# Float16 scores from the second group of batch 0 on, and a new written order of instructions

## The chip, the cores and the metric

The kernel runs on one core of one Trainium2 chip. The metric is the device time of one execution in microseconds (us). Three executions of the kernel before took 1048.6, 1049.95 and 1049.99 us; the median is 1049.95 us.

Five engines work side by side, each with an instruction stream of its own: PE (TensorE, matrix products into PSUM), DVE (VectorE), ACT (ScalarE), POOL (GpSimd) and SP (SyncE, which here issues most DMAs). An instruction waits for others by semaphores. PEld rows are PE's weight loads.

## The reference

Attention with pooled keys, then a soft mixture of experts over all tokens:

```python
kv_pool = kv.reshape(B, H // r, r, W // r, r, C).mean(axis=(2, 4))
k = v = kv_pool.reshape(B, -1, C) @ w_sr
s = (q @ k.transpose(0, 2, 1)) / sqrt(C);  a = softmax(s);  x = a @ v
logits = x @ phi                          # x is [B * N, 128], phi is [128, 32]
d = softmax over the tokens of logits;  slot_input = d.T @ x
slot_out[e] = relu(slot_input[e] @ w1[e]) @ w2[e]     # 8 experts, 4 slots each
out = softmax over the slots of logits @ slot_out
```

There are B = 4 batches of N = 12288 queries with C = 128 channels, and 768 pooled keys for each batch. All inputs and outputs are float32, and the queries are large, so scores and weights are computed in two parts, a high one and a low one that holds the rest.

## The kernel before, in words

The queries are cut into 96 blocks of 512, 24 for each batch, and into groups of 4 blocks (2048 queries), 6 for each batch. The last group is split 3 and 1. One block goes through these steps:

- ACT writes the high part of the block's queries (`q_hi`, L604 as float32r, L610 as float16), POOL the low part (`q_lo`, L615).
- PE computes the scores of 768 keys by 512 queries in 6 tiles, each as the sum of 3 products: high by high, low by high, high by low (`qk`, L625 to L627), 18 in all.
- DVE reduces them to one maximum for 32 queries (`rowmax1`, L643), folds the tiles (`rowmax2`, L653, L655), PE spreads the result (L663), DVE reduces again and transposes (L668, L673, the tile `mb`). There is one L673 in each block.
- DVE subtracts the maximum (`sub`, L681, into the tile `t`), ACT takes the exponential twice, as float16 (L689, `phi`) and as float32 (L693), POOL subtracts the two (`plo`, L698).
- PE multiplies by the values (L724, L725 with the high weights, L733 with the low ones), ACT brings the result to SBUF (L743).

After the four blocks of a group, group work computes logits, their running maximum over the tokens, and the slots' sums (`group_ops`, with L914 on PE, L827 on DVE, L877 and L892 on POOL). The row softmax over the slots has a maximum (L933), a subtraction, an exponential and a sum (`k_sum`, L950). For groups up to `SUMS` the sum stands in the loop, in two halves; for later ones it stands at the end, in one piece.

In batch 0 all scores are float32r (`HB = 1`: the first batch). From batch 1 on they are float16. That asks for more: the keys are divided by a power of two near their magnitude, and each group's queries too. For each group ACT makes two passes for the magnitude (`q_abs`, L534) and two that scale the queries in place (`q_mul`, L558), PE and DVE turn the magnitude into a power of two (`q_s_mm`, `q_s_g`), POOL multiplies it with the keys' (`q_sig`), and the exponentials and L655 take their scale from the tile that results (`qsg`) and not from a constant.

The keys of batches 1 to 3 are prepared while the batch before is computed (`kv_ops`: L453, L457, L462, L475, L496, L576, L577, L585), in the second half of its blocks.

The order on PE, DVE, ACT and POOL is written out by hand, by a planner in the program (`Plan`): each step is entered with an engine, a cost in us, a latency, a priority (the time at which it is wanted), what it depends on, and the buffers that it takes and gives back. The planner lets the engines run on those costs and picks at each step the ready one with the lowest priority; a `fill` step is held back for a gap until its due time, and a `hot` step is waited for a little. What it emits is the static order of each engine. `PER` is the planned time of one block, `HEAD` that of the first, and `act(n)` and `dve(n)` are costs by columns. The costs are no waits: on the chip each instruction starts when its semaphores allow.

At the end the experts' products are made, the last sums and reciprocals are finished, and 25 MB of output go out by SP's queue (`o_out`, `o_dma`).

Of the kernel before, what the change touches and what calls it, by code (L numbers as in the profile page):

```python
# [20 lines left out]
P = 128  # L21
# [6 lines left out]
HB = 1  # L28
# [8 lines left out]
SPARE = 0.02  # L37

# [4 lines left out]
class Plan:  # L43
# [170 lines left out]
def attention_then_soft_moe(ctx: ExitStack, tc: tile.TileContext, qT, kv0, kvT, w_sr, w_srT, phi, w1, w2, outT):  # L214
# [127 lines left out]
    PER = 9.8  # L342
# [11 lines left out]
    SUMS = 6  # L354
    JOIN = (0, AHEAD, 6, 8, 10, 13, 16, 19, EARLY)
    KV0 = 12.5
# [41 lines left out]
    def kv0_mm(h, c, first, end):  # L398
        if h == 0 and first:
            kT[0] = (  # L400
                bp.tile([P, NK], F32R, tag="khi", name="khi_0"),
                bp.tile([P, NK], F32R, tag="klo", name="klo_0"),
            )
# [156 lines left out]
    def sig(i):  # L560
        return SCALE if i < HB * BPB else QS[i // BPG]["s"][:, 0:1]
# [36 lines left out]
    def q_hi(i):  # L598
        if i < HB * BPB:
# [12 lines left out]
    def q_lo(i):  # L612
        hi, lo = qsp[i]
        eng = nc.gpsimd if i else nc.vector
        eng.tensor_tensor(out=lo, in0=q_src(i), in1=hi if i >= HB * BPB else hi.bitcast(F32), op=ALU.subtract)  # L615


    def qk(i, t):
        khi, klo = kT[i // BPB]
# [29 lines left out]
    def rowmax2(i):  # L649
# [6 lines left out]
            out=rq, in0=r1.unsqueeze(1).broadcast_to([P, NQD, NBK]), scalar=-math.log(PK) / SCALE if i < HB * BPB else QS[i // BPG]["s"][:, 1:2],  # L656
# [463 lines left out]
    kv_s(0, VBASE, VSTEP, m, [])  # L1120

    def group_ops(g):
# [22 lines left out]
        def bg(f=1.1):  # L1145
            return dve(n512) if fast else f * n512 / 512
# [4 lines left out]
        def go(name, eng, cost, dep, f, acq=(), use=(), path=None, fill=False):  # L1151
            k[0] += 1
            due = base + step * k[0] + (LATE if g else 4.0) if fill and not fast else None
            o[name] = op(eng, cost, 0.08, base + step * k[0], dep, lambda: f(g), acq=list(acq), use=[xl] + list(use) if name in ("0", "1v", "1l", "7m") else list(use), slack=0.0 if fast else SL, raw=0.05 if fast else 0.14, fill=due)
# [3 lines left out]
        else:  # L1158
            go("0", small, sm_(1), deps, g0)
            go("0r", "DVE", 0.21, [o["0"]], g0r, fill=True)  # L1160
            go("1u", small, sm_(1), [o["0r"]], g1u)
            go("1l", big, bg(), [o["1u"]], g1l)
        if g <= FAST:
            go("1v", small, sm_(2), [o["0r"]], g1v)
        if fast:
            go("2a", "DVE", dve(n512), [o["1l"]], lambda g: g2(g, 0, n16))
        else:
            go("2a", "DVE", dve(n512 // 2) + 0.06, [o["1l"]], lambda g: g2(g, 0, n16 // 2), fill=True)
            go("2a", "DVE", dve(n512 // 2) + 0.06, [o["2a"]], lambda g: g2(g, n16 // 2, n16), fill=True)
# [102 lines left out]
    for i in range(NB):  # L1272
# [5 lines left out]
        if o == 0 and g + 1 < NG and g + 1 >= HB * GPB:  # L1278
# [16 lines left out]
        ops["ql", i] = op("POOL" if i else "DVE", 1.28 if i else 0.65, 0.1, T0 - 0.9 * PER if i else -400.0, [a], lambda i=i: q_lo(i), use=[("q", g), ("qs", i)])  # L1295
        kd = [ops["k", b, x] for x in range(2 if b else 3)]
        for t in range(NT):
            u = t // 2
            if i == 0 and t == NT - 2:
# [4 lines left out]
                "PE", 3 * (0.2165 if f16_ else 0.2315), 0.17, T0 - QKP + 0.65 * t, [ops["ql", i]] + kd[: (1 if t < KSPLIT // P else 2) if b else t // 2 + 1] + ([ops["qk", i, t - 1]] if t else [ops["qk", i - 1, NT - 1]] if i else []),  # L1304
# [423 lines left out]
```

## Time and profile before

| | |
|---|---|
| profiled execution | 1051.33 us |
| its span, first to last instruction | 1049.5 us |
| median of the executions without profile | 1049.95 us |
| PE busy | 1013.4 us, 97% |
| DVE busy | 967.2 us, 92% |
| ACT busy | 892.6 us, 85% |
| POOL busy | 873.3 us, 83% |
| mean granted PE clock | 0.992 |

A row of instructions gives line, engine and operation, what is written from what, the shapes, and the count; behind it stand the busy time, the mean length in ns, and the idle time of the engine just before, with what ended it. Matrix products are pipelined: one that is listed with 0.38 us can start 0.22 us after the one before, so that the distance of starts, not the length, tells what it costs. The same holds in part for the other engines, whose instructions overlap a little at their ends. A stretch is given in us from the span's start.

### The profile page before, as it was taken

How to read it: one execution, taken by the hardware profiler on the slowest of the kernel's cores; microseconds unless marked ns; L12 is line 12 of the kernel's file. 1: busy time of each engine (PE TensorE's matmuls, PEld its weight loads, DVE VectorE, ACT ScalarE, POOL GpSimd, SP SyncE). 2: the span in 40 equal slices, each digit the busy share in tenths (PEclk: the TensorE clock that was granted, in tenths of full speed). 3: DMA queues.
4: the chain of work that ended last, by engine and by line, in shares of the span. 5: the costliest groups of instructions: out<-in, count | busy, mean ns of one | idle time of the engine just before them, and what ended most of it. 6: DMA issues, size and time to landing. Idle time of an engine off the chain costs nothing.

```text
span 1049.5 us, 24780 instructions
## 1 busy us (share of the span) xinstructions
PE 1013.4 (97%) x10297; PEld 774.2 (74%) x10297; DVE 967.2 (92%) x1487; ACT 892.6 (85%) x1185; POOL 873.3 (83%) x550
## 2 busy tenths in 40 slices
PE   8999999999999999999999999999999999998994
PEld 5788889888777767777777777777777777777452
DVE  6999999999999999999999999999999999997794
ACT  3777787889999998999999999999999999885473
POOL 0789999898899998899999999898998899985340
PEclk9999999999999999999999999999999999999997
DMA  9334411102116411111125303111100110113498
GB/s 370 116 65 98 101 37 51 42 1 102 42 16 146 101 34 54 42 31 71 42 46 117 90 13 86 42 61 42 42 7 36 42 41 2 42 41 122 179 417 366
DMA packets 15728, 89.16 MB, mean 85 GB/s; under 512 B 1664, under 2 KB 1920, under 8 KB 9344
## 3 DMA queue, kind: packets, MB, share of 16 engines
q1 hardware_dynamic: 11728, 69.47, 17.7%
q0 software_dynamic: 3312, 17.70, 8.9%
q8 instruction: 81, 1.33, 0.5%
q10 hardware_dynamic: 576, 0.41, 0.1%
q14 instruction: 31, 0.25, 0.1%
HBM read 58.87 MB, written 25.17 MB: 80 GB/s over the span
## 4 chain that ended last, share of the span: by engine, by line
PE 56%; DVE 31%; ACT 7%; DMA 3%; issue 3%; POOL 0%; DVEq 0%; SPq 0%; ACTq 0%
DVE t L681 11%; PE m L733 9%; PE m L724 9%; DVE r L643 9%; PE m L725 9%; PE s L625 8%; PE s L627 7%; PE s L626 7%; DVE mb L673 3%; ACT phi L689 3%; ACT t L693 2%; PE m L914 2%; DMA outT<-o 2%; DVE o L1562 1%; DVE m L653 1%
## 5 line engine op out<-in xcount | busy, mean ns | idle before, releaser
L698 POOL TENSOR_TENSOR plo<-t,phi 128x1536 f16<-128x1536 f32 x190 | 595.2, 3145 | 73.9 <-ACT t L693 69.8
L724 PE MATMUL m<-vhi,phi 128*128 128x161 f16 x2280 | 355.8, 234 | 2.6 <-ACT xl L743 1.5
L725 PE MATMUL m<-vlo,phi 128*128 128x160 f16 x2280 | 355.6, 233 | 0.0
L643 DVE TRANSPOSE_TENSOR_REDUCE r<-s 128x32 f32<-128x1024 f32 x289 | 346.4, 1225 | 8.4 <-PE s L627 4.5
L681 DVE TENSOR_TENSOR t<-s,mb 128x1024 f32<-128x1024 f32 (+1 forms) x384 | 343.6, 949 | 7.3
L724 PEld LDWEIGHTS <-phi 128*128 128x128 f16 x2304 | 224.8, 98 | 14.6 <-issue 7.9
L725 PEld LDWEIGHTS <-phi 128*128 128x128 f16 x2304 | 225.3, 98 | 11.1 <-issue 4.2
L689 ACT ACTIVATE phi<-t,qsg 128x1536 f16<-128x1536 f32 x144 | 223.4, 1569 | 3.4 <-DVE t L681 2.5
L625 PE MATMUL s<-qhi,khi 128*128 128x512 f16 (+1 forms) x574 | 222.6, 388 | 2.9 <-DVE t L681 2.4
L733 PE MATMUL m<-vhi,plo 128*128 128x161 f16 x2280 | 223.3, 234 | 0.0
L693 ACT ACTIVATE t<-t,qsg 128x1536 f32<-128x1536 f32 x144 | 222.2, 1563 | 0.2
L626 PE MATMUL s<-qlo,khi 128*128 128x512 f16 (+1 forms) x574 | 219.3, 382 | 0.6 <-POOL qlo L615 0.6
L627 PE MATMUL s<-qhi,klo 128*128 128x512 f16 (+1 forms) x574 | 219.5, 382 | 0.0
L733 PEld LDWEIGHTS <-plo 128*128 128x128 f16 x2304 | 173.1, 98 | 6.8 <-issue 6.4
L743 ACT ACTIVATE xl<-m 128x483 f32<-128x483 f32 (+1 forms) x189 | 81.5, 432 | 70.7 <-PE m L733 64.2
L615 POOL TENSOR_TENSOR qlo<-q,qhi 128x512 f16<-128x512 f32 (+1 forms) x95 | 117.6, 1238 | 23.8 <-ACT qhi L604 23.8
L627 PEld LDWEIGHTS <-klo 128*128 128x128 f16 x432 | 42.2, 98 | 51.8 <-issue 0.9
L625 PEld LDWEIGHTS <-khi 128*128 128x128 f16 x432 | 42.1, 97 | 50.1 <-DVE t L681 11.6
L689 ACT ACTIVATE phi<-t 128x1536 f16<-128x1536 f32 x48 | 70.7, 1475 | 9.1 <-DVE t L681 8.8
L673 DVE STREAM_TRANSPOSE mb<-m 128x512 f32<-128x512 f32 x96 | 68.3, 711 | 3.3
L693 ACT ACTIVATE t<-t 128x1536 f32<-128x1536 f32 x48 | 70.6, 1476 | 0.8
L626 PEld LDWEIGHTS <-khi 128*128 128x128 f16 x432 | 42.2, 98 | 38.7 <-issue 0.3
(215 smaller groups left out, 1117.2 us busy)
## 6 DMA issues: line engine op xcount, KB each, us to landing
q<-qT SPq DMA_DIRECT2D x23, 1024.0 KB, 4.9
outT<-o SPq DMA_DIRECT2D x22, 1024.0 KB, 7.0
kva<-kvT POOLq DMA_DIRECT2D x9, 1536.0 KB, 11.0
kva<-kvT SPq DMA_DIRECT2D x3, 1536.0 KB, 12.8
kv<-kv SPq DMA_DIRECT2D x6, 512.0 KB, 6.1
w<-w SPq DMA_DIRECT2D x2, 1536.0 KB, 7.0
w<-w SPq DMA_DIRECT2D x4, 768.0 KB, 4.9
kva<-kva POOLq DMA_DIRECT2D x3, 768.0 KB, 6.0
```

The costliest lines, as they stand in the source:

```text
L615: eng.tensor_tensor(out=lo, in0=q_src(i), in1=hi if i >= HB * BPB else hi.bitcast(F32), op=ALU.subtract)
L625: nc.tensor.matmul(s, khi[:, ks], hi, start=True, stop=False)
L626: nc.tensor.matmul(s, khi[:, ks], lo, start=False, stop=False)
L627: nc.tensor.matmul(s, klo[:, ks], hi, start=False, stop=True)
L643: nc.vector.tensor_reduce(out=MX[i][:, t : t + n, :].rearrange("p t b -> p (t b)"), in_=S[i, t // 2][:, u : u + n, :].rearrange("p t (b j) ...
L681: nc.vector.tensor_tensor(out=TT_[i, h][:, o : o + n, :], in0=S[i, t // 2][:, u : u + n, :], in1=MX[i].unsqueeze(1).broadcast_to([P, n, BQ ...
L689: nc.scalar.activation(hi, TT_[i, h], AF.Exp, scale=sig(i))
L693: nc.scalar.activation(t, t, AF.Exp, scale=sig(i))
L698: eng.tensor_tensor(out=lo, in0=TT_.pop((i, h)), in1=PP[i, h][0], op=ALU.subtract)
L724: nc.tensor.matmul(px, p, vhi[:, t, :], start=(t == 0 and (i >= AHD or part(i, k)[1] == 0)), stop=False)
L725: nc.tensor.matmul(px[:, 1:], p, vlo[:, t, :], start=False, stop=False)
L733: nc.tensor.matmul(px, PP[i, t // TH][1][:, t % TH, ks], vhi[:, t, :], start=False, stop=(t == NT - 1 and (i >= AHD or j == n - 1)))
```

## The change

It has four parts.

1. `HG = 1` takes the place of `HB = 1`: only the first group (blocks 0 to 3) has float32r scores; blocks 4 to 23 of batch 0 take the path that batches 1 to 3 take. So the magnitude and scaling steps come for groups 1 to 5 too. Batch 0's keys are held in both forms: the float32r ones (tiles `khi0`, `klo0`) and a float16 pair made from the float32 copy `pooled` (`k16_hi` on ACT, `k16_lo` on DVE), with the constants of `kv_c(0)`. `kv_v_out` no longer drops its entry, as its order against `kv_a` is free.
2. Costs in the planner are set anew, most of them lower: an exponential with a scale from a tile `act(1536) + 0.11` and not `+ 0.19`, float16 `q_lo` 1.13 and not 1.28, `q_abs` + 0.11 and not + 0.23, and small ones of the group work.
3. `PER` is 9.5 and not 9.8. Each step's priority is shifted by a number between -2.5 and 2.5 that is computed from the step's number and one entry of a list, by the stretch of 28 us (of planned time) that the priority falls in; entries that are 0 shift nothing.
4. `SUMS` is 9 and not 6: the sums of groups 6 to 8 stand in the loop, in halves.

```diff
-HB = 1
+HG = 1
...
+STRETCH = 28
+SHIFT = 2.5
+ORDERS = (
+    732519, 0, 228638, 630064, 412949, 395295, 489027, 282700, 709642, 260082, 106728, 749301, 343332, 514942,
...
+    343296, 625972, 183641, 0, 550532, 0, 0, 0, 0, 0, 0, 784859,
+)
+
+
+def shift(n, p):
+    w = min(max(int(p // STRETCH), 0), len(ORDERS) - 1)
+    if not ORDERS[w]:
+        return 0.0
+    x = (n * 7919 + ORDERS[w] * 104729) * 2654435761 % 2**32
+    x = (x ^ (x >> 15)) * 2246822519 % 2**32
+    x ^= x >> 13
+    return SHIFT * (2 * (x / 2**32) - 1)
...
         n = len(self.ops)
+        own = shift(n, prio)
         if eng != "PE" and any(ring == "m" for ring, _ in use):
             prio -= URGE
+        prio += own
...
-    PER = 9.8
+    PER = 9.5
...
-    SUMS = 6
+    SUMS = 9
...
+    K16 = 45.0
+    QA = 34.0
...
+    def k16_hi(h):
+        if h == 0:
+            kT[-1] = (
+                bp.tile([P, NK], F16, tag="khi", name="kh16_0"),
+                bp.tile([P, NK], F16, tag="klo", name="kl16_0"),
+            )
+        k0, k1 = KS[h]
+        nc.scalar.activation(kT[-1][0][:, k0:k1], pooled[0][:, k0:k1], AF.Copy, scale=VS[0][1][:, 0:1])
+
+    def k16_lo(h):
+        k0, k1 = KS[h]
+        hi, lo = kT[-1]
+        nc.vector.scalar_tensor_tensor(
+            out=lo[:, k0:k1], in0=pooled[0][:, k0:k1], scalar=VS[0][1][:, 0:1], in1=hi[:, k0:k1],
+            op0=ALU.mult, op1=ALU.subtract,
+        )
...
-        if i < HB * BPB:
+        if i < HG * BPG:
...
-        khi, klo = kT[i // BPB]
+        khi, klo = kT[i // BPB if i // BPB or i < HG * BPG else -1]
...
+    ops["kc", 0] = op("ACT", 0.6, 0.1, K16, [ops["vs", 0][1]], lambda: kv_c(0))
+    for h in range(2):
+        n = KS[h][1] - KS[h][0]
+        a = op("ACT", act(n) + 0.09, 0.1, K16 + h, [ops["vs", 0][1]], lambda h=h: k16_hi(h))
+        ops["k", -1, h] = op("DVE", dve(n), 0.08, K16 + h, [a], lambda h=h: k16_lo(h))
...
-        if o == 0 and g + 1 < NG and g + 1 >= HB * GPB:
+        if o == 0 and g + 1 < NG and g + 1 >= HG:
...
-                z.append(op("ACT", act(GQ // QH) + 0.23, 0.1, p + 0.6 * PER * j, [ops["q", g + 1]] + z[-1:], lambda g=g, j=j: q_abs(g + 1, j), use=qu, raw=0.0))
+                z.append(op("ACT", act(GQ // QH) + 0.11, 0.1, p + 0.6 * PER * j, [ops["q", g + 1]] + z[-1:], lambda g=g, j=j: q_abs(g + 1, j), use=qu, raw=0.0, at=QA))
...
-        f16_ = b >= HB
+        f16_ = g >= HG
...
-            e1 = op("ACT", act(TH * BQ) + (0.19 if f16_ else 0.1), 0.1, T0 + 6 + 3.2 * h, [se[h]] + sd, lambda i=i, h=h: exp_hi(i, h), acq=[("phi", (i, h))], use=[("t", (i, h))])
+            e1 = op("ACT", act(TH * BQ) + (0.11 if f16_ else 0.1), 0.1, T0 + 6 + 3.2 * h, [se[h]] + sd, lambda i=i, h=h: exp_hi(i, h), acq=[("phi", (i, h))], use=[("t", (i, h))])
```

## Rows read from the trace of the kernel before

**Rows 1.** Busy time by stretch: length, PE, PEld, DVE, ACT, POOL (instructions), clock, DMA share, GB/s.
```profile
64.30:139.80 75.50, 75.34 (x751) 67.01 (x751) 71.73 (x102) 59.22 (x68) 69.44 (x36) 1.00 0.42 92
139.80:260.70 120.90, 119.74 (x1219) 104.01 (x1217) 112.53 (x170) 102.70 (x145) 107.85 (x67) 1.00 0.17 50
260.70:376.40 115.70, 113.99 (x1210) 85.73 (x1209) 111.77 (x172) 108.24 (x137) 107.02 (x66) 1.00 0.30 70
376.40:494.90 118.50, 116.44 (x1216) 87.15 (x1214) 111.45 (x172) 111.86 (x154) 106.92 (x70) 1.00 0.17 51
494.90:609.00 114.10, 113.11 (x1204) 85.21 (x1202) 109.78 (x165) 107.52 (x138) 107.06 (x67) 1.00 0.31 71
609.00:727.60 118.60, 116.19 (x1220) 87.66 (x1218) 111.41 (x169) 111.60 (x154) 107.30 (x69) 1.00 0.17 51
727.60:936.10 208.50, 206.82 (x2211) 155.90 (x2209) 201.02 (x303) 192.89 (x246) 196.01 (x121) 1.00 0.09 32
```

**Rows 2.** The same stretches, first and last, counting DVE's L673 alone.
```profile
64.30:139.80 75.50, 5.69 (x8) 1.00 0.42 92
...
727.60:936.10 208.50, 15.65 (x22) 1.00 0.09 32
```

**Rows 3.** PE in order of time: start, length; score products of two blocks, first and after last.
```profile
103.49 0.48 PE L625 MATMUL s<-qhi,khi 128*128 128x512 f32 x1
...
107.72 0.24 PE L724 MATMUL m<-vhi,phi 128*128 128x161 f16 x1
...
825.28 0.38 PE L625 MATMUL s<-qhi,khi 128*128 128x512 f16 x1
...
829.17 0.23 PE L724 MATMUL m<-vhi,phi 128*128 128x161 f16 x1
...
834.30 0.38 PE L625 MATMUL s<-qhi,khi 128*128 128x512 f16 x1
```

**Rows 4.** Instructions by line, PE, group work (busy us, mean ns).
```profile
L914 PE MATMUL m<-xl,D 128*32 128x129 f32 x760 | 25.9, 276 | 1.6 <-ACT xl L743 0.9 <-POOL D L892 0.7
```

**Rows 5.** PE in order of time, batch 3, with the idle time before.
```profile
812.05 0.19 PE L663 MATMUL m<-rq,sel_h 128*128 128x64 f16 x1 [0.34 <-DVE rq L655]
```

**Rows 6.** Instructions by line, ACT: exponentials with and without tile scale, scaling, magnitude.
```profile
L689 ACT ACTIVATE phi<-t,qsg 128x1536 f16<-128x1536 f32 x144 | 223.4, 1569 | 3.4 <-DVE t L681 2.5
...
L689 ACT ACTIVATE phi<-t 128x1536 f16<-128x1536 f32 x48 | 70.7, 1475 | 9.1 <-DVE t L681 8.8
...
L558 ACT ACTIVATE q<-q,qg 128x1024 f32<-128x1024 f32 x36 | 40.1, 1137 | 2.4 <-DVE qg L548 2.4
L534 ACT ACTIVATE qj<-q 128x1024 fp8e4<-128x1024 f32 x36 | 37.7, 1046 | 0.0
```

**Rows 7.** ACT in order of time, batch 3: two and two exponentials.
```profile
825.68 3.05 ACT L689 ACTIVATE phi<-t,qsg 128x1536 f16<-128x1536 f32 x2
828.64 3.03 ACT L693 ACTIVATE t<-t,qsg 128x1536 f32<-128x1536 f32 x2
```

**Rows 8.** Instructions by line, DVE: row maximum's fold, low keys, row sums by halves.
```profile
L655 DVE SCALAR_TENSOR_TENSOR rq<-m,qsg,quad_h 128x64 f16<-128x64 f32 x72 | 20.4, 284 | 2.6
...
L655 DVE SCALAR_TENSOR_TENSOR rq<-m,quad_h 128x64 f16<-128x64 f32 x24 | 5.4, 224 | 0.8
...
L950 DVE TENSOR_REDUCE RM<-LL 128x8 f32<-128x256 f32 x12 | 4.8, 406 | 0.0
...
L462 DVE SCALAR_TENSOR_TENSOR klo<-m,kc,khi 128x512 f16<-128x512 f32 x3 | 2.2, 737 | 0.3 <-ACT khi L457 0.3
```

**Rows 9.** All engines in order of time near the last block: DVE and POOL.
```profile
953.40 1.78 DVE L698 TENSOR_TENSOR plo<-t,phi 128x1536 f16<-128x1536 f32 x1
...
953.53 1.77 POOL L894 TENSOR_TENSOR da<-da,sel 128x32 f32<-128x32 f32 x1
```

**Rows 10.** Instructions by line, POOL: the costliest.
```profile
L698 POOL TENSOR_TENSOR plo<-t,phi 128x1536 f16<-128x1536 f32 x190 | 595.2, 3145 | 73.9 <-ACT t L693 69.8 <-issue 1.6 <-PE s L627 0.9
```

**Rows 11.** DVE in order of time, at the start of the output.
```profile
982.35 0.68 DVE L950 TENSOR_REDUCE RM<-LL 128x16 f32<-128x512 f32 x1
```

More of the change, by code (lines that the diff above doesn't have):

```diff
@@ L400, in kv0_mm @@
             kT[0] = (
[L401 to L402 removed]
+                bp.tile([P, NK], F32R, tag="khi0", name="khi_0", bufs=1),
+                bp.tile([P, NK], F32R, tag="klo0", name="klo_0", bufs=1),
             )
@@ L1145, in bg, with go @@
         def bg(f=1.1):
-            return dve(n512) if fast else f * n512 / 512
+            return dve(n512) if fast else (f - 0.08) * n512 / 512
         o = {}
         k = [0]
-        def go(name, eng, cost, dep, f, acq=(), use=(), path=None, fill=False):
+        def go(name, eng, cost, dep, f, acq=(), use=(), path=None, fill=False, lat=0.08):
             k[0] += 1
             due = base + step * k[0] + (LATE if g else 4.0) if fill and not fast else None
-            o[name] = op(eng, cost, 0.08, base + step * k[0], dep, lambda: f(g), acq=list(acq), use=[xl] + list(use) if name in ("0", "1v", "1l", "7m") else list(use), slack=0.0 if fast else SL, raw=0.05 if fast else 0.14, fill=due)
+            o[name] = op(eng, cost, lat, base + step * k[0], dep, lambda: f(g), acq=list(acq), use=[xl] + list(use) if name in ("0", "1v", "1l", "7m") else list(use), slack=0.0 if fast else SL, raw=0.05 if fast else 0.14, fill=due)
         if g > FAST:
@@ L1158, in group_ops @@
         else:
-            go("0", small, sm_(1), deps, g0)
-            go("0r", "DVE", 0.21, [o["0"]], g0r, fill=True)
-            go("1u", small, sm_(1), [o["0r"]], g1u)
+            go("0", small, sm_(1) - (0.0 if fast else 0.09), deps, g0)
+            go("0r", "DVE", 0.14, [o["0"]], g0r, fill=True)
+            go("1u", small, sm_(1) - (0.0 if fast else 0.1), [o["0r"]], g1u)
             go("1l", big, bg(), [o["1u"]], g1l)
         if g <= FAST:
-            go("1v", small, sm_(2), [o["0r"]], g1v)
+            go("1v", small, sm_(2) - (0.0 if fast else 0.1), [o["0r"]], g1v)
         if fast:
@@ L1167, in group_ops @@
         else:
-            go("2a", "DVE", dve(n512 // 2) + 0.06, [o["1l"]], lambda g: g2(g, 0, n16 // 2), fill=True)
-            go("2a", "DVE", dve(n512 // 2) + 0.06, [o["2a"]], lambda g: g2(g, n16 // 2, n16), fill=True)
+            go("2a", "DVE", dve(n512 // 2) + 0.02, [o["1l"]], lambda g: g2(g, 0, n16 // 2), fill=True)
+            go("2a", "DVE", dve(n512 // 2) + 0.02, [o["2a"]], lambda g: g2(g, n16 // 2, n16), fill=True)
         if fast:
@@ L1174, in group_ops @@
             o["2"] = o["2a"]
-            go("2q", "POOL", 0.3, [o["2a"]], g2q)
+            go("2q", "POOL", 0.25, [o["2a"]], g2q)
         mc, md = ("m", ("pc", g)), ("m", ("pd", g))
@@ L1179, in group_ops @@
             go("2h", "ACT", 0.2, [o["2q"]], g2h)
-            go("2l", "POOL", 0.3, [o["2h"]], g2l)
+            go("2l", "POOL", 0.26, [o["2h"]], g2l)
             o["2q"] = o["2l"]
@@ L1191, in group_ops @@
         go("5e", "ACT", act(n512) + 0.13, [o["4"]], g5e, use=[dk])
-        go("5m", dbig, (bg() if g != FAST else 1.1 * n512 / 512) + 0.25, [o["5e"], o["1v"]], g5m, use=[dk])
+        go("5m", dbig, (bg() if g != FAST else 1.1 * n512 / 512) + 0.21, [o["5e"], o["1v"]], g5m, use=[dk])
         prev = [ops["g7", g - 1]] if g else []
         if g:
-            go("6r", "DVE" if fast else "ACT", 0.18 if fast else 0.3, [o["5m"]], g6r, fill=fast)
+            go("6r", "DVE" if fast else "ACT", 0.18 if fast else 0.21, [o["5m"]], g6r, fill=fast)
             prev = prev + [o["6r"]]
@@ L1294, in attention_then_soft_moe @@
         a = qh = op("ACT", act(BQ), 0.1, T0 - 1.0 * PER, qd + ([qh] if i else []) + ([ops["kb", 0]] if i == 2 else []) + ([ops["qr", 0]] if g == 0 and o else [ops["q", g]]), lambda i=i: q_hi(i), acq=[("qs", i)], use=[("q", g)])
-        ops["ql", i] = op("POOL" if i else "DVE", 1.28 if i else 0.65, 0.1, T0 - 0.9 * PER if i else -400.0, [a], lambda i=i: q_lo(i), use=[("q", g), ("qs", i)])
-        kd = [ops["k", b, x] for x in range(2 if b else 3)]
+        ops["ql", i] = op("POOL" if i else "DVE", (1.13 if f16_ else 1.25) if i else 0.65, 0.1, T0 - 0.9 * PER if i else -400.0, [a], lambda i=i: q_lo(i), use=[("q", g), ("qs", i)])
+        kd = [ops["k", b if b or not f16_ else -1, x] for x in range(2 if b or f16_ else 3)]
         for t in range(NT):
@@ L1381, in attention_then_soft_moe @@
         else:
-            a = [op("DVE", dve(n // KMP) + 0.05, 0.08, p, [ops["L", g]], lambda g=g, u=u: k_max(g, u), fill=p + 3 * PER) for u in range(KMP)]
+            a = [op("DVE", dve(n // KMP) + 0.03, 0.08, p, [ops["L", g]], lambda g=g, u=u: k_max(g, u), fill=p + 3 * PER) for u in range(KMP)]
         if g < FAST:
```

44 lines of the change are left out of this document (22 added, 22 removed), and 1 row of the table ORDERS.

## The prediction, made before the changed kernel was run

> **What bounds the kernel now.** I read the busy time by stretch first, cut where each block's transpose L673 starts; a block is 512 queries, and there is one L673 in each. In every stretch TensorE (PE) is busy for 98 to 100% and VectorE (DVE) for 93 to 97%; the granted clock is 1.00, the 2.4 GHz level, everywhere, so no stretch is explained by the clock [rows 1]. The same cut counted by L673 gives 8 blocks for the first stretch and 22 for the last [rows 2]; each of the five between holds 12. The pace is length over count: 9.44 us a block in blocks 4 to 11, 10.08 in 12 to 23 (the rest of batch 0), 9.64 and 9.88 in batch 1, 9.51 and 9.88 in batch 2, 9.48 in batch 3. The slow halves are those in which the next batch's keys and values are prepared; batch 3 has none to prepare.
>
> The second view is PE in order of time. The 18 score products of a block take 4.23 us in batch 0 (103.49 to 107.72, float32r) and 3.89 us later (825.28 to 829.17, float16). From there to the next block's first score product it is 834.30 - 825.28 = 9.02 us, in which PE starts one product behind the other and does no work for a group [rows 3]. A run of L914 every fourth block adds 25.9 us / (760/32) = 1.09 us, 0.27 a block [rows 4]. So PE alone needs 9.29 us a block, and batch 3 stands 0.19 above that. What lies between is small waits where PE meets DVE, as at 812.05: the row maximum's product idles PE for 0.34 us until DVE has finished L655 [rows 5]. PE is the bound, DVE is right behind it, and the order of the two decides how much of their slack shows.
>
> **Part 1: float16 scores in blocks 4 to 23.** On PE: 20 blocks at 4.23 - 3.89 = 0.34 us remove 6.8 us. ScalarE (ACT) pays: five groups get two magnitude passes of 1.05 us, two scalings of 1.14 us and one small instruction (at most as long as a scaling), 4.4 to 5.5 us a group; 20 blocks get four exponentials each, 0.09 us longer with a scale from a tile [rows 6]: 22 to 28 plus 7.5 us, with two key copies and the three constants some 32 to 38 us. ACT's idle time in the two stretches is 75.5 - 59.2 + 120.9 - 102.7 = 34.5 us [rows 1], so at today's length it would just fit. But the instructions overlap: four exponentials of 1.57 us start 825.68 to 828.64, 1.48 apart [rows 7], so some 0.09 of each added duration isn't time on the engine, and I count 28 us. That leaves ACT at about 97% in these blocks; in the second halves of batches 1 and 2 it is at 94%, with a pace of 9.88. Therefore I don't let blocks 12 to 23 go below that: 118.5 in place of 120.9 us, -2.4 us (ends: 0 if ACT takes it all back, -4.1 for the product alone). In blocks 4 to 11 DVE is the least loaded of all stretches, but the pace is already 9.44: 0 to -2.7, I take -0.8.
>
> **Part 2: the new order.** ACT's order was planned with 1.55 us for an exponential with a tile scale (1536/1200 + 0.08 + 0.19), while the trace shows 1.48 [rows 7]; the new plan has 1.47. Four a block make 0.3 us that ACT was believed busier than it is, so work was put late that could go early. First I bring each stretch to the best one of its kind: 24 to 35 from 115.7 to 12 x 9.48 = 113.7, -2.0; 48 to 59 from 114.1, -0.4; 60 to 71 -0.1; 36 to 47 nothing [rows 1]. That is -2.5. Second, the distance to PE's 9.29 is 0.19 x 90 blocks = 17 us if nothing waited any more. DVE forbids most of it: in batch 3 it is busy 201.0 / 22 = 9.14 us a block [rows 1], 0.15 under PE's need. I take a quarter, -4.3 (ends: 0, and -17; the shifts of up to 2.5 us that each instruction's priority gets can also cost, which is the last rival).
>
> **Part 3: DVE's new work.** L655 takes 0.284 in place of 0.224 us, 20 times: 1.2 us. Two tiny ones on each of five groups, no longer than an L655: at most 2.8. The low half of batch 0's float16 keys: 512 columns at 0.74 as L462 does it, 256 at no more than that: 1.2 to 1.5. Three groups' sums (SUMS 6 to 9) come from the end into the loop in halves: 6 x 0.41 = 2.4 [rows 8]. Together 5 to 8 us. DVE idles 75.5 - 71.7 + 120.9 - 112.5 = 12.2 us in blocks 4 to 23 and 7.1 us in 36 to 47 [rows 1], much of it in gaps that such work fills. I charge 0.5 (0 to 8: uncovered, it stands on the row-maximum path that PE waits for).
>
> The start has a price of its own. The new low half reads two tiles of SBUF on DVE, where L462 reads PSUM and one tile. The trace has one such meeting in the loop's last microseconds: from 953.40 DVE subtracts tiles for 1.78 us, and GpSimd's (POOL) product of only 32 elements a partition, begun at 953.53, takes 1.77 us, till DVE is done [rows 9]. In the other direction DVE would wait for a POOL instruction under way, most often plo's 3.15 us [rows 10]: two times 0 to 3.1. POOL is busy most of the time; I take 1.5 (0 to 6.3).
> The Trainium skill, SBUF — State Buffer, section "SBUF: two separate sides", says that a DVE instruction with two SBUF inputs and a GpSimd instruction that reads SBUF exclude each other for the whole instruction. The rows at 953 agree; by the rule alone the two halves could wait up to 3.1 us each, without it they cost their own 1.2 to 1.5 us.
>
> Also at the start, group 1's magnitudes, scaling and keys have to be ready before block 4: some 6 us of ACT between 34 and 60 us. ACT was 59.2 of 75.5 us busy just after [rows 1], so gaps of that size exist; nothing more is charged. If a gap is missed, block 4 is late by one exponential, 1.5 us.
>
> **Part 4: the end.** Of the sums that leave, one (0.68 us) stands just ahead of the second chunk's subtraction at 982.35 [rows 11]; most of the others waited there anyway. -0.3 (0 to -0.7). POOL's shorter float16 subtractions, the SP queue's loads (same order) and smaller cost constants move no time by themselves.
>
> **Sum:** -2.4 - 0.8 - 2.5 - 4.3 + 0.5 + 1.5 - 0.3 = -8.3 us. From the profiled execution's 1051.3 (1049.5 of span and 1.8 around it) this gives 1043.0; that execution stands 1.4 above the median of 1049.95, so for the median I say 1041.6.
>
> **Rivals.**
> A, the order is much better: DVE's 0.3 us gaps get filled, and the pace comes halfway to 9.29, -0.1 x 90 = -9 in place of -4.3 and part 1 in full (-6.8 in place of -3.2): 1049.95 - 16.6 = 1033. For it: three engines' planned durations move towards the rows. Against: DVE at 9.14 of 9.48. Chance 0.22.
> B, only the product counts: the old waits stay (parts 2 and 4 nothing), -3.2 + 2.0 = -1.2, or up to -4 if the key halves meet no POOL instruction; the middle is 1047.3. For it: batch 3's waits recur in every group alike, so they may follow from the durations and not from the plan. Chance 0.12.
> C, no change (within 0.2%, 2.1 us, which is what a measurement here can tell): gains eaten by 6.3 us at the start or by 8 us on DVE. Chance 0.07.
> D, slower, by one mechanism: shifted priorities put fill work of about 0.4 us on DVE ahead of the row maximum, and PE idles as at 812.05 [rows 5]. Place: blocks 24 to 94, 18 groups. Price 0.34 to 0.5 us each. Batch 3 has about one such wait a group; 8.3 us / (18 x 0.45) is one more a group, and there the gain is gone; with two more it is 1041.6 + 16 = 1058. For it: the shifts are large against DVE's slack of 0.34 us a block. Against: the order is made with waits known. Chance 0.12.
>
> The forecast (1036 to 1045) has 0.47. Faster by over 0.2%: 0.47 + 0.22 + 0.07 of B = 0.76; same 0.07 + 0.05 of B = 0.12; slower 0.12. The range 1029 to 1053 takes in A's centre, B, C and the mild half of D.
>
> **What would show it.** Score products 0.216 us apart from block 4; blocks 12 to 23 at 9.6 to 9.9 with ACT at 95% or more; L673's pace in batch 3 at 9.40 to 9.46, and the wait before L663's product shorter or rarer; the new DVE subtraction of keys stretched beyond 0.8 us when plo runs. Wrong if batch 3's pace rises above 9.48, if blocks 0 to 4 get over 2 us longer, or if blocks 12 to 23 stay at 10.

## The result and the profile after

The changed kernel takes 1034.21 us (median of 4 executions, 1032.88 to 1035.5), the kernel before in the same job 1049.28 (1048.56 to 1049.99). The ratio is 0.9856, with a 95% interval of 0.9839 to 0.9873: 15.1 us faster. The profiled execution took 1035.5 us with a span of 1033.3; before it was 1051.33 and 1049.5. Executions differ with TensorE's granted clock: those of the kernel before have spans of 1046.4 to 1047.0 us or are 1 to 3 us longer, the profiled one among the longer by a lower clock near its end that is shown further down, and one execution of the kernel with float32r products below took 1451.52 us at a mean granted clock of 0.661 and is left out of its ratio, though not of its median.

Lines have moved: of the loop's lines before, most are 38 higher now (L673 is L711, L625 to L627 are L663 to L665). First the page of the changed kernel: busy time of each engine, its share of the span, and the instructions.

```profile
span 1033.3 us, 24829 instructions
PE 1004.6 (97%) x10309; PEld 743.8 (72%) x10309; DVE 967.8 (94%) x1502; ACT 921.9 (89%) x1225; POOL 870.8 (84%) x555
```

ACT has 29 us more work than before, DVE 0.6 more, PE 9 less. Now the windows by stretch of the changed kernel, cut at L711 as [rows 1] were at L673, with the same columns. The first line, blocks 0 to 3, is new; the next seven answer to the seven lines of [rows 1].

```profile
27.60:67.80 40.20, 37.76 (x288) 29.30 (x287) 36.58 (x49) 36.09 (x44) 26.57 (x15) 0.92 0.16 62
67.80:141.70 73.90, 73.54 (x764) 55.42 (x763) 71.42 (x106) 68.48 (x83) 69.75 (x40) 1.00 0.47 104
141.70:257.70 116.00, 116.00 (x1219) 87.39 (x1217) 112.61 (x174) 112.87 (x155) 106.96 (x67) 1.00 0.14 46
257.70:371.70 114.00, 113.76 (x1207) 85.07 (x1205) 111.05 (x173) 108.36 (x138) 106.95 (x67) 1.00 0.31 71
371.70:487.30 115.60, 115.44 (x1217) 87.14 (x1215) 112.44 (x176) 112.97 (x157) 106.07 (x68) 1.00 0.19 53
487.30:600.40 113.10, 113.00 (x1205) 85.03 (x1203) 109.62 (x167) 107.19 (x136) 108.32 (x68) 1.00 0.31 71
600.40:716.70 116.30, 116.06 (x1221) 87.57 (x1219) 111.02 (x169) 112.48 (x154) 106.11 (x69) 1.00 0.18 52
716.70:924.50 207.80, 207.41 (x2212) 155.85 (x2210) 201.15 (x305) 193.91 (x247) 195.57 (x123) 1.00 0.09 31
```

Read length against PE's busy time. From block 24 to 94 (the last five lines) the lengths sum to 666.8 us and PE's work to 665.7: 1.1 us of idle time are left. In [rows 1] the same five were 675.4 and 666.55, with 8.85 us idle. PE's work is the same to 0.9 us; what went is idle time. (Busy time is not a fixed amount: two other orders below do the same products in 670.0 and 670.7 us of it.) In blocks 4 to 23 it is the other way round: 196.4 became 189.9 us, and PE's work fell from 195.1 to 189.5. There was 1.3 us of idle time before, so 5.5 of the 6.5 us gained are work taken off PE.

By the exact starts of L673 and L711 the two profiled spans differ thus: start to block 0 +0.5, blocks 0 to 3 +2.9, 4 to 11 -1.5, 12 to 23 -5.0, batch 1 -4.5, batch 2 -3.4, blocks 72 to 95 -1.2, from there to the first output -3.4, output -0.7; together -16.2 us.

The view of who waited for whom, PE alone, blocks 24 to 94 (us in total, times, longest): the kernel before, its four largest rows, and then the only row of the changed kernel.

```profile
PE m L663 <- DVE rq L655: 3.8, 10, 0.8
PE s L625 <- DVE t L681: 1.3, 3, 0.6
PE m L914 <- ACT xl L743: 0.9, 2, 0.5
PE m L724 <- ACT xl L743: 0.7, 1, 0.7
```

```profile
PE m L701 <- DVE rq L693: 0.4, 2, 0.2
```

The row maximum's product, whose wait [rows 5] showed once, waited ten times for 3.8 us; now it waits twice for 0.4. (A few more rows of before bring the total to 8.2.)

PE in order of time in the changed kernel, block 8, three score products: start, length.

```profile
106.77 0.38 PE L663 MATMUL s<-qhi,kh 128*128 128x512 f16 x1
106.99 0.38 PE L664 MATMUL s<-qlo,kh 128*128 128x512 f16 x1
107.20 0.38 PE L665 MATMUL s<-qhi,kl 128*128 128x512 f16 x1
```

The starts are 0.216 us apart on average, and 18 products take 3.89 us (106.77 to 110.66) where the first line of [rows 3] began 4.23.

### The profile page after: what moved, and what is told of

Same layout as the page of the kernel before. It is cut to its first block, busy times and chain, and to the rows that moved or that the text cites. A ratio compares the mean times of both kernels' runs of the same rounds, so it can differ in the third digit from the quotient of the medians.

```text
span 1033.3 us, 24829 instructions
## 1 busy us (share of the span) xinstructions
PE 1004.6 (97%) x10309; PEld 743.8 (72%) x10309; DVE 967.8 (94%) x1502; ACT 921.9 (89%) x1225; POOL 870.8 (84%) x555
## 4 chain that ended last, share of the span: by engine, by line
PE 65%; DVE 22%; ACT 5%; POOL 3%; DMA 3%; issue 2%; DVEq 0%; SPq 0%; ACTq 0%; POOLq 0%
PE m L771 11%; PE m L762 11%; PE m L763 11%; PE s L663 9%; PE s L664 9%; PE s L665 9%; DVE t L719 7%; DVE r L681 7%; PE m L952 2%; ACT phi L727 2%; DVE mb L711 2%; DMA outT<-o 2%; POOL plo L736 1%; ACT t L731 1%; DVE o L1605 1%
## 5 line engine op out<-in xcount | busy, mean ns | idle before, releaser
L727 ACT ACTIVATE phi<-t,qsg 128x1536 f16<-128x1536 f32 x184 | 286.0, 1568 | 7.2 <-DVE t L719 5.9
L731 ACT ACTIVATE t<-t,qsg 128x1536 f32<-128x1536 f32 x184 | 286.2, 1567 | 1.5
L663 PE MATMUL s<-qhi,khi 128*128 128x512 f16 (+1 forms) x454 | 174.3, 384 | 0.5
L664 PE MATMUL s<-qlo,khi 128*128 128x512 f16 (+1 forms) x454 | 172.8, 381 | 0.0
L665 PE MATMUL s<-qhi,klo 128*128 128x512 f16 (+1 forms) x454 | 172.6, 380 | 0.0
L653 POOL TENSOR_TENSOR qlo<-q,qhi 128x512 f16<-128x512 f32 (+1 forms) x95 | 114.7, 1207 | 23.6 <-ACT qhi L642 23.6
L665 PEld LDWEIGHTS <-klo 128*128 128x128 f16 x432 | 42.2, 98 | 51.1
L663 PEld LDWEIGHTS <-khi 128*128 128x128 f16 x432 | 42.1, 97 | 46.5 <-DVE t L719 9.6
L711 DVE STREAM_TRANSPOSE mb<-m 128x512 f32<-128x512 f32 x96 | 68.3, 711 | 3.3
L648 ACT ACTIVATE qhi<-q 128x512 f16<-128x512 f32 x92 | 56.9, 619 | 0.3
L596 ACT ACTIVATE q<-q,qg 128x1024 f32<-128x1024 f32 x46 | 52.4, 1138 | 4.7 <-DVE qg L586 4.7
```

Of the source, the lines that this page charges most:

```text
L653: eng.tensor_tensor(out=lo, in0=q_src(i), in1=hi if i >= HG * BPG else hi.bitcast(F32), op=ALU.subtract)
L663: nc.tensor.matmul(s, khi[:, ks], hi, start=True, stop=False)
L664: nc.tensor.matmul(s, khi[:, ks], lo, start=False, stop=False)
L665: nc.tensor.matmul(s, klo[:, ks], hi, start=False, stop=True)
L727: nc.scalar.activation(hi, TT_[i, h], AF.Exp, scale=sig(i))
L731: nc.scalar.activation(t, t, AF.Exp, scale=sig(i))
```

## The experiments

The stretches below are from one profiled execution of each kernel, in us, by the starts of L673 or its descendant. "4-23" are the blocks with the float16 change, "24-94" (from block 24's start to block 94's) those whose products are the same in all kernels. The ratio is to the kernel before, run in the same job. The recorded expectations for shifts in one half give 567, 578 and 570 to 590 us for blocks 24 to 94, which is 100 us too low: the table has 666.8 with all shifts and 678.4 without.

| kernel | blocks 0-3 | 4-23 | 24-94 | median | ratio to before |
|---|---|---|---|---|---|
| before | 37.3 | 196.4 | 675.4 | 1049.28 | 1 |
| changed | 40.1 | 189.9 | 666.8 | 1034.21 | 0.9856 |
| float16 alone, old plan | 42.5 | 200.2 | 673.4 | 1055.33 | 1.005 |
| no shifts | 37.5 | 194.2 | 678.4 | 1049.56 | 1.0001 |
| other numbers | 37.5 | 199.1 | 680.2 | 1056.01 | 1.0056 |
| new plan, old float32r, no shifts | 37.3 | 199.0 | 674.6 | 1050.63 | 1.0017 |
| shifts early only | 38.9 | 189.9 | 680.4 | 1048.75 | 1.0005 |
| shifts late only | 38.7 | 194.2 | 676.7 | 1046.77 | 0.998 |
| one cost 0.005 higher | 39.0 | 195.1 | 680.6 | 1053.88 | 1.0044 |
| changed order, float32r products | 37.7 | 196.8 | 666.8 | 1041.36 | 0.9926 |
| low keys on POOL (second run) | 37.0 | 189.9 | 666.5 | 1032.88 | 0.9844 |

### Part 1 alone

The kernel before with float16 scores from block 4 on, its costs, `PER` and `SUMS` as they were. The switch is shown; the code of the change's first part comes with it.

```diff
-HB = 1
+HG = 1
...
```

> Float16 scores from block 4 on, with the planner of the kernel before (its costs, PER 9.8, no shift, SUMS 6). Theory 1 (product and order each give their part): blocks 4 to 23 gain 3 to 5 us of the 6.5 that the whole change gained there, because the old costs still misplace work on a fuller ACT; batches 1 to 3 stay within 2 us of before; the start loses 2 to 3 us: 1045 to 1049 us. Rival (the gain in blocks 4 to 23 is the product alone): 6 to 7 us there, 1043 to 1045. Rival 2 (without a new order, ACT takes it all back): 1050 or more.

Measured: 1055.33 us, ratio 1.005 (1.0036 to 1.0065). Slower, where my theory expected a gain; it is the second rival's outcome. The windows of this kernel for blocks 0 to 3, 4 to 11 and 12 to 23, columns as above:

```profile
27.06:69.53 42.47, 38.79 (x321) 30.87 (x321) 37.83 (x48) 36.13 (x45) 28.62 (x15) 0.96 0.16 63
69.53:151.93 82.40, 76.07 (x737) 54.32 (x735) 72.71 (x109) 71.03 (x86) 70.78 (x42) 0.98 0.46 98
151.93:269.71 117.78, 115.86 (x1215) 86.62 (x1213) 112.50 (x175) 111.92 (x152) 105.83 (x67) 1.00 0.12 42
```

Blocks 12 to 23 gain 3.2 us, but PE idles 6.3 us in blocks 4 to 11 (82.40 less 76.07) and the first two stretches lose 12 us together, against 37.3 and 75.5 before. PE's longest wait there is for the row maximum behind DVE's new subtraction of keys, which this plan puts 0.4 us after the start of a POOL subtraction (the last section shows it):

```profile
47.45 0.19 PE L682 MATMUL m<-rq,sel_h 128*128 128x64 f16 x1 [2.94 <-DVE rq L674]
```

A part of the loss is the clock, which is 0.57 from 47.4 to 51.4 and again from 143 to 147. What follows: the new instructions, laid out by the old plan, cost more than the cheaper products give.

### No shifts, and other shifts

The changed kernel, once with `SHIFT = 0.0`, once with each entry of the list raised by one, which draws other numbers of the same size.

```diff
-SHIFT = 2.5
+SHIFT = 0.0
```

> The whole change, but no priority is shifted (SHIFT 0). Theory 1 (the planner's costs, now near the trace, make the order better): batches 1 to 3 keep some 6 of the 9 us that they gained, total 1035 to 1039 us. Rival (the shifts do it, the costs nothing): batches 1 to 3 come back to within 2 us of before, total 1042 to 1046.

```diff
-    x = (n * 7919 + ORDERS[w] * 104729) * 2654435761 % 2**32
+    x = (n * 7919 + (ORDERS[w] + 1) * 104729) * 2654435761 % 2**32
```

> The whole change, with every number of the list one higher: shifts of the same size, other values. If the listed numbers are a fitted choice: slower than without any shift, 1038 to 1050, with waits of PE on DVE spread through all stretches. If any shift does as well: within 2 us of 1034.

Measured: without shifts 1049.56 us, ratio 1.0001 (0.9991 to 1.001); with other numbers 1056.01, ratio 1.0056 (1.0041 to 1.0071). Both are outside what was expected of them (at most 1046 and 1050). So the whole gain of 15 us needs the shifts, and not any shifts: the one other list that was tried, with numbers of the same size, loses 6 us against none. The waits of PE in the kernel without shifts, blocks 24 to 94, its two largest rows:

```profile
PE m L701 <- DVE rq L693: 4.0, 6, 2.5
PE s L663 <- DVE t L719: 1.5, 4, 0.5
```

It is the row-maximum wait again, the largest, that the chosen numbers bring to 0.4 us. But the waits are only a part of the difference. The windows of blocks 24 to 94 without shifts and with other numbers:

```profile
258.90:937.30 678.40, 669.98 (x7053) 502.61 (x7052) 643.74 (x983) 633.68 (x829) 624.65 (x390) 1.00 0.19 51
...
263.70:943.90 680.20, 670.68 (x7053) 501.61 (x7052) 644.45 (x982) 633.19 (x828) 624.46 (x390) 1.00 0.19 51
```

Against the changed kernel's 666.8 us the first is 11.6 longer: 7.3 of idle time (8.4 for 1.1) and 4.3 of busy time for the same products. Without shifts the clock also fell to 0.57 in one stretch, from 461 to 465; with other numbers it didn't in these blocks, and the busy time is as long.

### The new plan without float16

The changed kernel with `HG = 6`, so that all of batch 0 is float32r, without the float16 keys and without shifts: the new costs, `PER` and `SUMS` alone.

```diff
-HG = 1
+HG = 6
...
-SHIFT = 2.5
+SHIFT = 0.0
```

> Float32r scores in all of batch 0 (as before), with the new costs, PER 9.5, SUMS 9, no shift. Against the run without shift it gives the worth of float16 by itself under the new planner. Theory 1: blocks 4 to 23 are 5 to 7 us longer than there, the start 2 to 3 us shorter, batches 1 to 3 alike: 1038 to 1043 us. Rival (ACT takes the product's gain back): no longer than the run without shift.

Measured: 1050.63 us, ratio 1.0017 (1.0005 to 1.0029). That is outside the 1038 to 1043 of the theory: costs that stand nearer to the trace, with `PER` and `SUMS`, give nothing by themselves. In blocks 4 to 23 float16 is worth 199.0 - 194.2 = 4.8 us here, but blocks 24 to 94, whose instructions are the same in both, then differ by 3.8 us the other way (674.6 and 678.4), some of it the stretch at 461.

### Shifts in one half of the list only

Windows 0 to 8 of the list are the first 252 us of planned time, about batch 0.

```diff
-    if not ORDERS[w]:
+    if not ORDERS[w] or w >= 9:
```

> The whole change, shifts only in the first nine stretches of the list (planned time below 252 us, about batch 0). If each stretch's number was chosen for that stretch and acts there: blocks 4 to 23 as with all shifts (about 190 us), later ones near the run without shift (24 to 94: 578 us, against 567 with all): 1044 to 1047 us. Rival (a shift acts on all that comes later): later stretches anywhere from 570 to 590.

```diff
-    if not ORDERS[w]:
+    if not ORDERS[w] or w < 9:
```

> The whole change, shifts only from the tenth stretch on (planned time from 252 us). If the numbers act each in its own stretch whatever came before: blocks 24 to 94 about 567 us, blocks 0 to 23 as without shift (232): 1037 to 1040 us. Rival (they were chosen for the very state that the earlier stretches leave): blocks 24 to 94 at 575 to 590 us, total 1046 to 1058.

Measured: early only 1048.75 us, ratio 1.0005 (0.9995 to 1.0014); late only 1046.77, ratio 0.998 (0.9971 to 0.999). The early numbers alone bring blocks 4 to 23 to the full 189.9 us, and leave blocks 24 to 94 at 680.4, no better than without shifts (678.4), so the total is above the 1044 to 1047 expected. The late numbers alone bring blocks 24 to 94 to 676.7 us, not to 666.8: most of their effect is gone when the blocks ahead of them are laid out another way. So the two halves don't add up; later numbers fit the state that the earlier ones leave.

### A cost changed by five nanoseconds

The planned cost of both exponentials with a tile scale (the second is shown), 0.005 us higher; everything else, the list too, as in the changed kernel.

```diff
-            e2 = op("ACT", act(TH * BQ) + (0.11 if f16_ else 0.1), 0.1, T0 + 7.6 + 3.2 * h, [e1], lambda i=i, h=h: exp_t(i, h), use=[("t", (i, h))], raw=0.13)
+            e2 = op("ACT", act(TH * BQ) + (0.115 if f16_ else 0.1), 0.1, T0 + 7.6 + 3.2 * h, [e1], lambda i=i, h=h: exp_t(i, h), use=[("t", (i, h))], raw=0.13)
```

> The whole change, with one planned cost moved by 0.005 us (an exponential with a tile scale 0.115 in place of 0.11). If the listed numbers fit this one plan and nothing near it: most of the gain goes, 1042 to 1056 us. If they are good orders in themselves: within 3 us of 1034.

Measured: 1053.88 us, ratio 1.0044 (1.0029 to 1.0059). The gain is gone, and blocks 24 to 94 take 680.6 us. The higher cost is about as near to the trace (1.475 us planned where 0.11 gives 1.47; the starts of such exponentials are 1.48 us apart in [rows 7], and 1.47 in the median of 110 pairs). But it gives another schedule, for which the numbers were not chosen. That is the plainest sign that the list is a fit to one schedule. (Some 1.7 us of the profiled execution, in blocks 12 to 23, go to a clock of 0.57 from 239.5 to 243.5: an estimate, 0.43 of 4 us.)

### The same order with the old products

The changed kernel's order kept instruction for instruction; in blocks 4 to 23 alone the queries' parts and the keys of the score products are float32r. These blocks read the keys not divided by the power of two, so their scores are in another scale.

```diff
-        if i < HG * BPG:
+        if i < BPB:
...
-        khi, klo = kT[i // BPB if i // BPB or i < HG * BPG else -1]
+        khi, klo = kT[i // BPB]
```

> The changed kernel's order, instruction by instruction, but blocks 4 to 23 make their score products in float32r (from batch 0's unscaled float32r keys, so the scores of these blocks come out in another scale; all work on ACT, DVE and POOL stays). It prices the float16 product alone, in the order found for it. Theory: PE is the bound in these blocks, so the 0.34 us a block come back nearly whole: blocks 4 to 23 take 196 to 198 us in place of 189.9, total 1039 to 1042 us. Rival (the order left room that hides it): less than 3 us longer.

Measured: 1041.36 us, ratio 0.9926 (0.9906 to 0.9946). Its windows for blocks 4 to 11, 12 to 23 and 24 to 94:

```profile
65.46:141.86 76.40, 75.95 (x765) 67.41 (x763) 72.16 (x107) 69.65 (x83) 71.82 (x40) 1.00 0.46 101
141.86:262.25 120.39, 120.30 (x1219) 103.19 (x1217) 113.51 (x174) 113.43 (x156) 108.38 (x67) 1.00 0.13 44
...
262.25:929.10 666.85, 665.70 (x7049) 500.74 (x7047) 645.30 (x988) 634.69 (x828) 623.02 (x391) 1.00 0.20 52
```

Blocks 4 to 23 are 196.8 us, 6.9 over the changed kernel's 189.9; the prediction's arithmetic for the products was 20 x 0.34 = 6.8. From block 24 to block 94 the two kernels agree to 0.1 us. So in this order the float16 product gives back all of its arithmetic and nothing else. The order gives the other gain, that in blocks 24 to 94; the tail is read apart, below.

### The low keys on POOL

The subtraction of batch 0's float16 keys moved from DVE to POOL, at its place in the order; ACT divides the keys in place first, so that POOL has two plain inputs. It ran twice, the second time on one chip with the changed kernel run again.

```diff
-        nc.scalar.activation(kT[-1][0][:, k0:k1], pooled[0][:, k0:k1], AF.Copy, scale=VS[0][1][:, 0:1])
+        nc.scalar.activation(pooled[0][:, k0:k1], pooled[0][:, k0:k1], AF.Copy, scale=VS[0][1][:, 0:1])
+        nc.scalar.activation(kT[-1][0][:, k0:k1], pooled[0][:, k0:k1], AF.Copy)
...
-        nc.vector.scalar_tensor_tensor(
-            out=lo[:, k0:k1], in0=pooled[0][:, k0:k1], scalar=VS[0][1][:, 0:1], in1=hi[:, k0:k1],
-            op0=ALU.mult, op1=ALU.subtract,
-        )
+        nc.gpsimd.tensor_tensor(out=lo[:, k0:k1], in0=pooled[0][:, k0:k1], in1=hi[:, k0:k1], op=ALU.subtract)
```

> The whole change and its order, but the low half of batch 0's float16 keys is subtracted on POOL (ACT scales the float32 copy in place first), so no DVE instruction with two SBUF inputs stands in the start. Theory (DVE's subtraction was held by POOL, PE idled behind it and its clock fell): blocks 0 to 3 take 37 to 38.5 us in place of 40.15, the clock stays at 1.00 around 49 us, total 1031 to 1033. Rival (the added ACT work makes the loss, or the order there): 40 us or more, total 1034 or above, as ACT has two instructions more.

> The changed kernel again, beside the next one: 1032 to 1035 us, blocks 0 to 3 at 40 us with the clock falling near 49 us.

> The version with the keys' low half on POOL again: 1 to 3 us below the changed kernel on the same chip, 1030 to 1033 us, blocks 0 to 3 at 37 us, the clock at 1.00 from 40 to 60 us.

Measured: 1032.17 us, ratio 0.9846 (0.983 to 0.9863), and 1032.88, ratio 0.9844 (0.9829 to 0.9859); the changed kernel beside the second one 1033.98, ratio 0.9855 (0.984 to 0.987). All engines in order of time in the changed kernel: start, length, and in brackets the idle time of the engine before.

```profile
43.80 3.12 POOL L736 TENSOR_TENSOR plo<-t,phi 128x1536 f16<-128x1536 f32 x1 [1.82 <-ACT t L731]
45.78 1.68 DVE L458 SCALAR_TENSOR_TENSOR kl<-pooled,inv,kh 128x512 f16<-128x512 f32 x1
...
47.74 0.23 DVE L693 SCALAR_TENSOR_TENSOR rq<-m,quad_h 128x64 f16<-128x64 f32 x1
...
48.02 0.20 PE L701 MATMUL m<-rq,sel_h 128*128 128x64 f16 x1 [1.42 <-DVE rq L693]
```

While POOL's subtraction runs until 46.92, DVE's instruction of 512 columns stands for 1.68 us, where the prediction counted 0.74, and ends 0.54 us after POOL's; the row maximum behind it is late, and PE idles 1.42 us. The Trainium skill, SBUF — State Buffer, section "SBUF: two separate sides", says that a DVE instruction with two SBUF inputs and a GpSimd instruction that reads SBUF exclude each other; the 1.68 us agree. With the subtraction on POOL, the same place:

```profile
45.56 0.33 DVE L689 TENSOR_REDUCE m<-r 128x16 f32<-128x96 f32 x1 [1.01 <-ACT xl L779]
45.99 1.79 POOL L459 TENSOR_TENSOR kl<-pooled,kh 128x512 f16<-128x512 f32 x2
...
46.20 0.20 PE L699 MATMUL m<-rq,sel_h 128*128 128x64 f16 x1 [0.92 <-DVE rq L691]
```

Here DVE comes to the row maximum as soon as ACT lets it, after 1.01 us of idle time, and PE idles 0.92 us all the same. So of the 1.42 us about 0.5 are the lock. The blocks' starts say so too: from block 1's transpose to block 2's it is 10.44 to 10.45 us in the three traces with this order and DVE's subtraction, and 9.93 in both with POOL's. What this is worth has to be read with the clock. The windows of the changed kernel around 49 us:

```profile
40.00:48.90 8.90, 7.16 (x59) 5.85 (x57) 8.83 (x13) 6.96 (x8) 6.05 (x4) 1.00 0.35 121
48.90:52.40 3.50, 3.50 (x25) 3.31 (x23) 3.50 (x7) 2.99 (x4) 3.50 (x3) 0.52 0.00 0
```

PE idled 1.42 us, and from 48.90 the granted clock is 0.52, the 1.2 GHz level, for 3.5 us. A stretch like it, from 28.6 us, is also in this trace. In the second trace of the changed kernel only the earlier one recurs (blocks 0 to 3: 39.1 us), and in the kernel with float32r products, which has the same 1.69 us on DVE and the same 1.42 us of idle time, neither does (37.7 us). In both traces with the keys on POOL there is none, and blocks 0 to 3 take 37.0. PE's idle time ahead of the earlier stretch, 1.07 to 1.09 us at 27 us, is in all five of these traces, with the fall and without it. So the lock itself costs 0.5 to 0.6 us (37.66 less 37.03 for blocks 0 to 3), and the clock up to 2.5 more (40.14 less 37.66), not in every execution. Of the changed kernel run again I had expected 40 us with the fall near 49; it had neither. The medians are 1.1 us apart on the same chip; the intervals overlap, so that the version with POOL is faster is likely and not shown.

## Why the prediction held, and where it did not

The time is within the range, and it is not that of the forecast but of rival A, whose sum was 1033: an order that lets the product count whole and takes PE's waits away. Its two sizes came (-9 and -6.8 named, -8.6 and -6.5 measured); its reason, that planned durations move towards the rows, did not, as Part 2 shows. And there is luck in the sum: the start and the tail, where 1.7 us were forecast (0.5 and 1.5 in Part 3, -0.3 in Part 4), came to +3.4 and -4.0, mostly by the clock in single executions, and cancel. Step by step:

**The bound.** PE as the bound with DVE's row maximum behind it was right: the waits that went are those of L663 on L655 [rows 5]. But the floor of 9.29 us a block was wrong, and with it the 17 us "if nothing waited". It was built of one block without group work and L914 [rows 3, 4], and left out the groups' other products. PE's rows in batch 3 of the kernel before, by line:

```profile
L860 PE MATMUL m<-cb,sel_bf 128*128 128x64 bf16 x10 | 1.1, 193 | 0.0
L542 PE MATMUL m<-qab,ones 128*128 128x1 bf16 x10 | 1.0, 165 | 0.0
```

They are at most 2.1 us in 22 blocks, 0.10 a block. The busy time of PE in [rows 1] was a better floor, 206.82 / 22 = 9.40 us in batch 3. By that reading there were 8.85 us to win from block 24 to 94, where the result took 8.6. In the changed kernel batch 3 runs at 9.45, inside the 9.40 to 9.46 named, with PE busy for 99.8%.

**Part 1, -3.2 forecast.** Measured -6.5 (196.4 to 189.9), with 6.9 us for the product in the fixed order. The mis-sized term is what ACT takes back: 3.6 us were charged, because ACT would be at about 97% in blocks 12 to 23. ACT is there at 112.87 of 116.0, 97%, as forecast, and it costs PE nothing: PE is busy in all of 116.00 us. A loaded ACT needn't cost time if its work is laid where nobody waits for it. In the old plan the same float16 scores made blocks 4 to 23 longer by 3.8 us (200.2), a part of it by the clock, and which of the new instructions did the rest was not separated; in the new plan without shifts they gave 4.8 of 6.8. So what is taken back depends on the order, from about 10 us to nothing.

One reading in this part was wrong. Exponentials with a tile scale start 1.48 us apart, and so the prediction took their added 0.09 us for no time on the engine. But those with a constant scale overlap as much; ACT in order of time, kernel before, batch 0:

```profile
105.83 1.48 ACT L693 ACTIVATE t<-t 128x1536 f32<-128x1536 f32 x1
107.20 1.47 ACT L689 ACTIVATE phi<-t 128x1536 f16<-128x1536 f32 x1
108.58 0.62 ACT L604 ACTIVATE qhi<-q 128x512 fp32r<-128x512 f32 x1
```

They start 1.37 and 1.38 us apart, so the 0.09 us are time on the engine, about 7 us in the 80 exponentials. ACT had idle time for them. Blocks 12 to 23 came to 9.66 us each, inside the 9.6 to 9.9 named.

**Part 2, -6.8 forecast.** Measured -8.6 in blocks 24 to 94. The size is near, the reason failed: "work was put late that could go early" because the planned exponential was 1.55 us and the trace shows 1.48 [rows 7]. The new costs without shifts gave 1050.63 us, and with float16 1049.56: no gain. The gain comes from the numbers of the list, and these were priced only as a possible cost. That is the step that failed: the planned durations were taken for the cause, and in their place it is the fitted shifts. The first half of the term, "each stretch to the best one of its kind", fits by stretch only in part: blocks 24 to 35 came to 114.0 us (113.7 named), but 36 to 47 gained 2.9 and 60 to 71 gained 2.4 where nothing and 0.1 were named.

**Rivals D and B.** Shifts that don't fit do cost time: with other numbers blocks 24 to 94 take 680.2 us, with the cost nudged 680.6, against 675.4 before. That is 5 us, not the 16 of rival D's price, and not in the changed kernel. Its mechanism, more waits for the row maximum, isn't borne out. PE's waits there, with other numbers and then with the cost nudged:

```profile
PE m L701 <- DVE rq L693: 2.1, 5, 0.9
PE s L663 <- DVE t L719: 1.6, 4, 0.6
```

```profile
PE s L663 <- DVE t L719: 4.3, 8, 1.1
PE m L701 <- DVE rq L693: 2.4, 8, 0.9
```

The row maximum costs less than the 3.8 us before. Idle time is 9.5 and 10.7 us for 8.85, and the rest is busy time (670.7 and 669.9 for 666.5); what lengthens it is open. In rival B, -1.2 without the 1.5 us of the key halves is -2.7, not -4, so its middle would be nearer to 1048.

**Part 3.** The start was charged with 1.5 us and measured +3.4, 0.5 of it before block 0. The place was right: DVE's new subtraction met POOL's and stood for 1.68 us. Its size was over-charged, it is 0.5 to 0.6 us; what was missing is the lower clock in two stretches of the profiled execution, up to 2.5 us. "Over 2 us longer" was named as a sign against the forecast; it came, in that execution, by this. DVE's other new work costs nothing that can be seen: its busy share rose in blocks 4 to 23, and PE doesn't wait.

**Part 4, -0.3 forecast.** -4.0 measured in the profiles, from the last block on. Most of it isn't the change. The windows of the tail, a piece at full clock and then the piece with the first slots' products, before:

```profile
963.90:966.90 3.00, 1.30 (x33) 0.76 (x32) 1.34 (x8) 1.25 (x5) 1.04 (x2) 1.00 0.32 55
966.90:973.00 6.10, 5.50 (x26) 1.50 (x26) 4.76 (x11) 1.79 (x5) 4.20 (x5) 0.50 0.26 106
```

and after:

```profile
951.80:954.80 3.00, 2.08 (x38) 1.24 (x36) 2.25 (x12) 1.66 (x5) 0.69 (x2) 1.00 0.00 0
954.80:960.00 5.20, 4.88 (x44) 2.00 (x48) 5.09 (x15) 2.26 (x5) 4.53 (x6) 1.00 0.47 154
```

Before, this piece ran at a clock of 0.50, and after at 1.00, and its 16 products took 3.64 us and 1.92:

```profile
968.14 3.64 PE L1434 MATMUL ph<-w,sm 128*32 128x512 f32 x16 [0.27 <-DVE sm L1411]
```

```profile
955.53 1.92 PE L1477 MATMUL ph<-w,sm 128*32 128x512 f32 x16 [0.27 <-DVE sm L1454]
```

I read [rows 1], which end at 936, and wrote that the clock was 1.00 in every stretch; the tail was not among them. The lower clock there doesn't come from the old `SUMS`: from the last block to the first output transfer it is 38.4 us before and 35.0 after, and the kernel with float16 alone, which has the old `SUMS`, takes 35.5 and that without shifts 35.7, both at full clock, while the one with `HG = 6` and the new `SUMS` takes 38.7 with a clock of 0.5 from about 969. By the first of these the change itself is worth some 0.5 us there, near the forecast. So of the 16.2 us between the profiled spans about 3 are the clock in the tail; by the medians, where executions with stretches of lower clock are on both sides, the difference is 15.1.

What stays open: the fitted order without ACT's float16 work was not tried, since that order is fitted to a plan that holds these instructions. How much the order alone is worth can be said only as in the table, 8.6 us in blocks 24 to 94. And whether a fit to the float32r plan would reach the same idle time of 1.1 us isn't known.

## What to carry to other kernels

Take as an engine's floor its busy time in the stretch, not a sum of the products that you can name; the idle time that remains is about what an order can win (a little more, as the same products were listed with 665.7 to 670.7 us of busy time), and where it is 1 us in 196 it is mostly work taken off the engine that helps. When a change holds a list of fitted numbers, ask how much idle time there is to fit away, and price the list by that and not by its reasons; every later edit, even of a cost by 0.005 us, then needs the fit again. And read the clock to the end of the span, tail included.

## What the runs showed of the hardware

- The same instructions on the same engines, in orders that differ by shifts of at most 2.5 us, took 1034 to 1056 us; in blocks 24 to 94 alone 666.8 to 680.4, of which PE's busy time is 665.7 to 670.7.
- A float16 score product of 512 columns is worth 6.9 us in 360, 0.019 us each, against float32r, in an order in which PE idles for about 0.5 us of 190.
- DVE's subtraction of 512 columns from two SBUF tiles stood 1.68 us in the changed kernel, and 3.22 us with the old plan, which put it 0.4 us behind the start of POOL's instruction. DVE in order of time, with float16 alone:

```profile
43.69 3.22 DVE L439 SCALAR_TENSOR_TENSOR kl<-pooled,inv,kh 128x512 f16<-128x512 f32 x1
```

  The blocked time is shown as a long instruction, not as idle time, so that DVE seems busy.
- After PE idled 1.42 us at 48 us the granted clock fell to 0.52 in one trace and stayed at 1.00 in two others with the same order and the same idle time; after 1.07 to 1.09 us of idle time at 27 us it fell in two traces of five.
- An exponential of 1536 columns with its scale from a tile is 0.09 us longer than one with a constant scale, by the distance of starts (1.48 and 1.38 us) as by the listed length (1.57 and 1.48).
